# Pair 2's weights and combinations made during the first two pairs of an attention and two-layer kernel, with a rewritten step order and seam

## The chip, the cores and the metric

One core of one Trainium2 chip runs the whole program. The metric is the device time in microseconds (us); lower is better. Engine names are those of the profile: PE (TensorE matmul), PEld (its weight loads), DVE (VectorE), ACT (ScalarE), POOL (GpSimd), SP (SyncE, which issues the DMAs).

## The reference

Rotary attention over 2 batches of 8 heads, 576 positions of 64 values, and then two feed-forward layers over the 1152 tokens (512 values, 2048 hidden). The arithmetic is float32.

```python
attn = softmax(rotate(q) @ rotate(k).T / sqrt(D))     # per head
x = (attn @ v).transpose(0, 2, 1, 3).reshape(1152, 512)
h = x @ w_in                                          # layer 1
x = where(h > 0, h, exp(min(h, 0)) - 1) @ w_out       # elu
h = x @ w2_in                                         # layer 2
out = (h * tanh(softplus(h))) @ w2_out                # mish
```

## The kernel before

Each float32 operand is held as two parts, a rounded high part (a copy by ACT into type fp32r) and a low part (the difference, by DVE or POOL), and each product is three matmuls: high by high, low by high, high by low. XH and XL are the two parts of the layers' input, [128, 4, 1152] (512 values as 4 blocks of 128, then the tokens).

The hidden values of a layer are cut into 16 blocks of 128, taken as 8 pairs. Pairs 0 and 1 of layer 1 are computed plainly, in six units (2 pairs by 3 chunks of 384 tokens): `unit_step(n)` makes `g1_mm` (24 matmuls), `elu` (two ACT passes out of PSUM), `elu_join` (DVE), `elu_hi` (ACT), `elu_lo` (DVE). Units 0 to 2 begin in the end of the attention. After each two units four output tiles wait in `pend`; `g3_mm` makes one (`g2_mm`, 12 matmuls into one of two `ps_h` banks), and `g3_y` copies it into the accumulator Y on ACT.

Pairs 2 to 7 of layer 1 use a scheme of seven products in place of eight. A product `mm(k)`, written P1 to P7 in the step's order, multiplies a combination of weight blocks (a11, a12, s1, a22, s3, s2, s4) with a combination of input blocks (b11, b21, b22 of the input itself, and t1, t2, t3, t4), 12 matmuls of 288 columns. The products accumulate in three PSUM places: "a" and "b" (tag s, two buffers) and "c". The combinations t1 to t4 exist for both batches (u = 0, 1). They are made once, `form1` (three or two elementwise passes of 576 columns out of XH and XL), then `put_hi` (ACT) and `lo1`. t1 is put over a quarter of XH and XL, so it must come after the last unit's matmuls. Pair 2's weight combinations are the object `w2` (class `Pieces`): `load` (an ACT pass out of the raw DMA buffer), `bits` (two or three DVE passes), `sums` (four DVE passes), `round` (high part on ACT, low part on POOL or DVE). `first_pieces(n)` spreads all this over units 2 to 5.

A step of pairs 2 to 7 is the list `STEP`, worked off from left to right by `layer_step`. It is one order for all engines; each engine's queue keeps it, and semaphores join them. P: product; c, d: bank copied out by ACT, or added by DVE, into a temporary (m1, u2, m5, u3, s); e, x, h, l: elu (two ACT passes), join (DVE), high part (ACT), low part; X, K, L: join, high and low part of the previous pair's s; H: one of 12 output tiles of the previous pair (6 matmuls of 384 columns); Y: its sum into Y on DVE; w, p, s, r: load, bits, sums and rounding of the next pair's weights; o, or: bits and rounding of this pair's output weights; a: load of the next output weights. Entries that begin with j have no action. `BY` names the engine of the low parts. In the first step there is no previous pair, and `or0` drains the four output tiles left over in `pend`. A load takes one of three raw buffers, whose next DMA is issued when the last bits pass has read it.

After the sixth step `seam` makes the last pair's 12 output tiles, the high and low parts of the new input (XH, XL from Y), the next weights and combinations; `second` then computes layer 2: three plain chunks (`classic`), then steps of its own order.

Of the kernel before, what the change touches and what calls it, by code (L numbers as in the profile page):

```python
# [14 lines left out]
ALU = mybir.AluOpType  # L15
# [11 lines left out]
def kernel(  # L27
# [196 lines left out]
    def tmp(tag):  # L224
        return late_pool[0].tile([128, 2 * CH], F32, tag=tag, name=tag, bufs=4)

    def tmps():
# [3 lines left out]
        return tmp("ta")  # L231
# [705 lines left out]
    def moe(mp, early):  # L937
# [96 lines left out]
        def g3_y():  # L1034
# [15 lines left out]
        pend, queue1, sums1 = [], [], []  # L1050
# [38 lines left out]
        def unit_step(n):  # L1089
# [35 lines left out]
        def first_pieces(n):  # L1125
            D, G = nc.vector, nc.gpsimd
            if n == 2:
                for u in range(2):
                    for k in range(3):
                        form1(u, "t1", k, G)  # L1130
            elif n == 3:
                for k in range(3):
                    form1(0, "t3", k, G)
                put_hi(0, "t3")
                lo1(0, "t3", G)
                w2.load(0)
                w2.bits(0, 0, 1, 2)
            elif n == 4:
                for k in range(2):
                    form1(0, "t2", k, G)  # L1140
                w2.load(1)
                w2.bits(1, 0, 1, 2)
                put_hi(0, "t2")
                lo1(0, "t2", G)
                for k in range(2):
                    form1(0, "t4", k, D)
                put_hi(0, "t4")
                lo1(0, "t4", D)
                for k in range(3):
                    form1(1, "t3", k, G)  # L1150
                w2.sums(0, 1)
            elif n == 5:
                w2.sums(2, 3)
                w2.round(0)
                w2.round(2)
                put_hi(1, "t3")
                w2.round(3, D)
                w2.round(1, D)
                lo1(1, "t3", D)
                for k in range(2):  # L1160
                    form1(1, "t2", k, D)
                put_hi(1, "t2")
                lo1(1, "t2", G)

# [6 lines left out]
        class Pair:  # L1171
# [28 lines left out]
            def temp(self, nm):  # L1200
                if nm not in self.t:
                    if nm == "s":
                        x = second_pool[0].tile([128, S], F32, tag="sx", name="sx", bufs=1)
# [593 lines left out]
```

## Time and profile before

| | us |
|---|---|
| runs shown, median of 2 (595.70 and 596.48) | 596.09 |
| the profiled execution | 595.98 |
| its span, first to last instruction | 594.2 |
| PE busy in the span | 547.0 |
| DVE busy | 434.5 |
| ACT busy | 341.4 |
| POOL busy | 246.1 |

The profile is of one execution, so a stretch or a wait is read against its span of 594.2 us and its own time of 595.98. Busy time is by engine; the engines run beside each other, so it does not add up to the span. In the trace the attention lies before 158 us, pairs 0 and 1 up to 189.4, the six steps from there to 364.3, the seam up to 391.6 and layer 2 behind it.

### The profile page before, as it was taken

How to read it: one execution, taken by the hardware profiler on the slowest of the kernel's cores; microseconds unless marked ns; L12 is line 12 of the kernel's file. 1: busy time of each engine (PE TensorE's matmuls, PEld its weight loads, DVE VectorE, ACT ScalarE, POOL GpSimd, SP SyncE). 2: the span in 40 equal slices, each digit the busy share in tenths (PEclk: the TensorE clock that was granted, in tenths of full speed). 3: DMA queues.
4: the chain of work that ended last, by engine and by line, in shares of the span. 5: the costliest groups of instructions: out<-in, count | busy, mean ns of one | idle time of the engine just before them, and what ended most of it. 6: DMA issues, size and time to landing. Idle time of an engine off the chain costs nothing.

```text
span 594.2 us, 9329 instructions
## 1 busy us (share of the span) xinstructions
PE 547.0 (92%) x3436; PEld 491.6 (83%) x3436; DVE 434.5 (73%) x736; ACT 341.4 (57%) x640; POOL 246.1 (41%) x196
## 2 busy tenths in 40 slices
PE   9999999999996486999999998596999999999997
PEld 6788888888996386999999997485998988998986
DVE  6677777786635836687887877489688878887764
ACT  4766667787643438476665754355766466455530
POOL 7999989424495304132442323053022132222300
PEclk9999999999999679799999999798999999999999
DMA  6878889644202031314123140210332413213004
GB/s 221 224 179 201 217 217 267 143 138 153 72 0 72 1 107 36 107 35 142 45 98 106 37 142 4 103 36 1 107 107 71 133 48 103 82 61 107 1 1 159
DMA packets 49405, 60.70 MB, mean 102 GB/s; under 512 B 20944, under 2 KB 38736, under 8 KB 48592
## 3 DMA queue, kind: packets, MB, share of 16 engines
q1 hardware_dynamic: 48816, 59.52, 34.3%
q10 hardware_dynamic: 544, 0.59, 0.3%
q8 instruction: 27, 0.44, 0.3%
q14 instruction: 18, 0.15, 0.1%
HBM read 46.92 MB, written 2.36 MB: 83 GB/s over the span
## 4 chain that ended last, share of the span: by engine, by line
PE 77%; DVE 12%; ACT 5%; POOL 3%; issue 2%; DMA 1%; DVEq 0%; ACTq 0%; SPq 0%; POOLq 0%
PE ps_s L1190 23%; PE ps_h L1438 17%; PE ps_h L1028 10%; PE ps_s L478 8%; PE psA L598 7%; PE psT L558 5%; PE ps_h L1011 2%; POOL Y L1083 2%; DVE Y L1042 1%; DVE ta L1239 1%; DVE ta L1083 1%; DVE ws L906 1%; PE ps_s L211 1%; POOL ta L1083 1%; PE psA L667 1%
## 5 line engine op out<-in xcount | busy, mean ns | idle before, releaser
L1210 ACT ACTIVATE ta<-ps_s 128x576 f32<-128x576 f32 x52 | 33.2, 651 | 77.7 <-PE ps_s L1190 77.7
L490 DVE TENSOR_REDUCE mn<-ps_s 128x1 f32<-128x576 f32 x71 | 53.5, 757 | 23.8 <-PE ps_s L478 23.4
L1448 DVE TENSOR_TENSOR Y<-Y,ps_h 128x512 f32<-128x512 f32 (+1 forms) x64 | 43.5, 679 | 26.9 <-PE ps_h L1438 26.6
L512 ACT ACTIVATE P<-ps_s,mn 128x576 f32<-128x576 f32 x71 | 52.4, 739 | 10.7 <-DVE mn L490 9.5
L129 POOL TENSOR_TENSOR wo0bl<-wu,wo0bh 128x512 fp32r<-128x512 f32 x15 | 20.5, 1374 | 89.5 <-ACT wo0bh L128 47.5
L129 POOL TENSOR_TENSOR wo0l<-wu,wo0h 128x512 fp32r<-128x512 f32 x16 | 21.7, 1368 | 78.1 <-ACT wo0h L128 61.4
L1028 PE MATMUL ps_h<-gg,wo0bh 128*128 128x384 f32 x144 | 40.5, 361 | 12.3 <-DVE Y L1042 10.6
L1438 PE MATMUL ps_h<-wo0h,gg 128*128 128x512 f32 x144 | 46.5, 404 | 5.6 <-ACT Y L1446 3.4
L1042 DVE TENSOR_TENSOR Y<-Y,ps_h 128x384 f32<-128x384 f32 x72 | 39.1, 550 | 15.9 <-PE ps_h L1028 15.4
L1438 PE MATMUL ps_h<-wo0bh,gg 128*128 128x512 f32 (+2 forms) x148 | 45.7, 390 | 0.0
L558 PE MATMUL psT<-idn,P 128*128 128x128 f32 x288 | 42.9, 273 | 0.0
L1028 PEld LDWEIGHTS ps_h<-gg,wo0bh 128*128 128x128 f32 x144 | 27.4, 201 | 15.1 <-DVE Y L1042 12.5
L1028 PE MATMUL ps_h<-gg,wo0h 128*128 128x384 f32 x144 | 37.3, 340 | 2.8 <-DVE Y L1042 2.8
L578 ACT ACTIVATE pt<-psT 128x512 f32<-128x512 f32 x40 | 23.8, 594 | 26.0 <-PE psT L558 25.8
L1438 PEld LDWEIGHTS ps_h<-wo0h,gg 128*128 128x128 f32 x144 | 26.6, 192 | 11.5 <-ACT Y L1446 3.9
L598 PE MATMUL psA<-pt,v_t 128*64 128x256 f32 (+1 forms) x240 | 35.9, 401 | 0.0
L558 PEld LDWEIGHTS psT<-idn,P 128*128 128x128 f32 x288 | 34.7, 141 | 1.3 <-DVE mn L490 0.4
L1214 DVE TENSOR_TENSOR ta<-ta,ps_s 128x576 f32<-128x576 f32 x26 | 19.5, 752 | 21.7 <-PE ps_s L1190 21.4
L1438 PEld LDWEIGHTS ps_h<-wo0bh,gg 128*128 128x128 f32 x148 | 26.9, 188 | 5.5 <-DVE Y L1448 0.2
L112 DVE TENSOR_SCALAR wv<-wv 128x512 int32<-128x512 int32 x28 | 14.5, 516 | 22.0 <-ACT wv L96 22.0
L1190 PE MATMUL ps_s<-XH,wi1h 128*128 128x288 f32 x96 | 22.1, 313 | 8.1 <-ACT wi1h L128 8.1
L1438 PE MATMUL ps_h<-wo0l,gg 128*128 128x512 f32 x72 | 29.0, 402 | 0.0
(261 smaller groups left out, 1751.2 us busy)
## 6 DMA issues: line engine op xcount, KB each, us to landing
raw<-in_w_in_dram SPq DMA_DIRECT2D x32, 512.0 KB, 3.7
raw<-in_w_out_dram SPq DMA_DIRECT2D x32, 512.0 KB, 3.7
qk_t<-in_qk_dram SPq DMA_DIRECT2D x6, 1152.0 KB, 5.6
qa<-qh SPq DMA_DIRECT2D x28, 144.0 KB, 3.3
out_dram<-Y SPq DMA_DIRECT2D x8, 256.0 KB, 2.0
ka<-kh SPq DMA_DIRECT2D x14, 144.0 KB, 4.6
ka<-kl SPq DMA_DIRECT2D x14, 144.0 KB, 4.2
qb<-ql SPq DMA_DIRECT2D x14, 144.0 KB, 2.7
```

Of the source, the lines that this page charges most:

```text
L129: (by or nc.gpsimd).tensor_tensor(out=lo, in0=u, in1=plain(hi), op=ALU.subtract)
L478: nc.tensor.matmul(third[j] if us[k] == 2 else psS[us[k]][:, j, :HS], lhsT=l, rhs=r(slice(j * HS, j * HS + HS)), start=(a == 0), stop=(a = ...
L490: nc.vector.tensor_reduce(out=m[:, 0:1], in_=psS[u][:, :, :HS], axis=AX.XY, op=ALU.min)
L512: nc.scalar.activation(out=P.rearrange("p (j n) -> p j n", j=2), in_=s[:, :, :HS], func=AF.Exp, scale=-1.0, bias=m, accum_out=sm_t[p, g][: ...
L558: nc.tensor.transpose(tv[:, c, :], P[:, k:k + 128], idn)
L598: nc.tensor.matmul(o[64 * h:64 * h + 64, cols], lhsT=v, rhs=rhs, start=(c == 0 and first), stop=(c == 4), skip_group_check=True,)
L1028: nc.tensor.matmul(o, lhsT=w[:, e * 128:e * 128 + 128], rhs=x, start=(k == 0), stop=(k == 5))
L1042: nc.vector.tensor_tensor(out=y, in0=y, in1=o, op=ALU.add)
L1190: nc.tensor.matmul(self.o[r][:, u, :H2], lhsT=w[i][:, cc, :], rhs=XO[u][xn][x][:, cc, :], start=(first and n == 0), stop=(last and n == 3 ...
L1210: nc.scalar.activation(out=self.temp(nm), in_=self.bank(r), func=AF.Copy)
L1438: nc.tensor.matmul(o, lhsT=l, rhs=w[:, es], start=(k == 0), stop=(k == 5))
L1448: nc.vector.tensor_tensor(out=y, in0=y, in1=o, op=ALU.add)
```

## The change

The temporaries: tag ta had four buffers of 768 columns, shared by elu, the combinations and the steps, with a buffer of its own for s; now ta has five buffers of 576 and a tag tc one buffer of 768 for elu and the plain chunks of layer 2.

Units: the outputs in `pend` are made one before the join and three before the low part, from unit 2 on. `first_pieces`: t3, t2 and t4 go from POOL to DVE for the most part; w2's load, bits, sums and rounding begin at unit 2; all of t4 is made within unit 5. `STEP` and `BY` are new lists with the same entries; the last step also makes the bits of the next output weights behind their load. `seam`: loads and bits of the weights first, the output weights rounded at once, each g3_y one output behind, the low part of XL one output later than its high part, sums, t3 and t2 inside the loop.

```diff
     def tmp(tag):
-        return late_pool[0].tile([128, 2 * CH], F32, tag=tag, name=tag, bufs=4)
+        n, bufs = (S, 5) if tag == "ta" else (2 * CH, 1)
+        return late_pool[0].tile([128, n], F32, tag=tag, name=tag, bufs=bufs)
...
                 nc.scalar.activation(out=XH[part], in_=Yf[part], func=AF.Copy)
-                (nc.vector if e == 1 or t < 1 else nc.gpsimd).tensor_tensor(
-                    out=XL[part], in0=Yf[part], in1=plain(XH[part]), op=ALU.subtract
-                )
+                late_xl.append((t, e, part))
+            elif late_xl:
+                last_xl()
+
+        def last_xl():
+            t, e, part = late_xl.pop(0)
+            (nc.gpsimd if t and e == 1 else nc.vector).tensor_tensor(
+                out=XL[part], in0=Yf[part], in1=plain(XH[part]), op=ALU.subtract
+            )
...
+                outs(1)
                 o = elu_join(*o)
                 if n == 5:
                     lo1(0, "t1", nc.vector)
                     lo1(1, "t1", nc.vector)
-            if o is not None:
                 o = elu_hi(*o)
-            if n >= 3:
-                outs(4)
-            if o is not None:
+                outs(3)
                 elu_lo(*o)
             first_pieces(n)
...
             if n == 2:
-                for u in range(2):
-                    for k in range(3):
-                        form1(u, "t1", k, G)
+                w2.load(0)
+                w2.load(1)
+                for k in range(3):
+                    form1(0, "t1", k, G)
+                for k in range(3):
+                    form1(0, "t3", k, D)
+                w2.bits(0, 0, 1, 2)
+                w2.bits(1, 0, 1, 2)
+                for k in range(3):
+                    form1(1, "t1", k, G)
+                for k in range(2):
+                    form1(0, "t2", k, D)
             elif n == 3:
-                for k in range(3):
-                    form1(0, "t3", k, G)
+                for k in range(2):
+                    form1(0, "t4", k, D)
+                w2.sums(0, 1, 2, 3)
+                put_hi(0, "t4")
+                lo1(0, "t4", D)
+                w2.round(0)
+                w2.round(1, D)
                 put_hi(0, "t3")
                 lo1(0, "t3", G)
...
                 put_hi(0, "t2")
                 lo1(0, "t2", G)
...
+            elif n == 4:
                 for k in range(3):
-                    form1(1, "t3", k, G)
-                w2.sums(0, 1)
-            elif n == 5:
-                w2.sums(2, 3)
-                w2.round(0)
-                w2.round(2)
-                put_hi(1, "t3")
-                w2.round(3, D)
-                w2.round(1, D)
-                lo1(1, "t3", D)
+                    form1(1, "t3", k, D)
                 for k in range(2):
                     form1(1, "t2", k, D)
+                put_hi(1, "t3")
+                w2.round(2)
+                lo1(1, "t3", D)
+                w2.round(3, D)
                 put_hi(1, "t2")
                 lo1(1, "t2", G)
+            elif n == 5:
+                for k in range(2):
+                    form1(1, "t4", k, D)
+                put_hi(1, "t4")
+                lo1(1, "t4", D)
...
         STEP = (
-            "o00", "P1", "Js", "o10", "Xs", "w0", "cm1", "o01", "p00", "Ks", "P5", "Ls",
-            "p01", "P6", "P2", "cu2", "dm1", "H0", "cm5", "or0", "Y0", "o11", "r0", "H1",
-            "w1", "H2", "em1", "P3", "P7", "cu3", "Y1", "H3", "Y2", "jm1", "p10", "du2",
-            "xm1", "H4", "p11", "d22", "hm1", "P4", "H5", "H6", "s3", "eu2", "Y3", "ju2",
-            "s1", "H7", "xu2", "s2", "eu3", "Y4", "or1", "Y5", "H8", "ju3", "s4", "xu3",
-            "a0", "r1", "Y6", "hu3", "cs", "H9", "Y7", "hu2", "lm1", "H10", "Y8", "Y9",
-            "H11", "Y10", "lu3", "lu2", "Y11", "r3", "r2", "a1", "es",
+            "Js", "P1", "w0", "o00", "cm1", "o01", "P5", "P6", "Xs", "o10", "p00", "Ks",
+            "Ls", "o11", "P2", "or0", "cu2", "H0", "H1", "w1", "p01", "or1", "p10", "dm1",
+            "cm5", "P7", "em1", "jm1", "P3", "Y0", "H2", "p11", "H3", "Y1", "xm1", "s3",
+            "H4", "hm1", "s1", "du2", "Y2", "s2", "H5", "Y3", "cu3", "s4", "H6", "a0",
+            "lm1", "Y4", "H7", "eu2", "Y5", "r1", "P4", "ju2", "xu2", "d22", "r2", "hu2",
+            "eu3", "r0", "H8", "H9", "Y6", "H10", "Y7", "r3", "ju3", "H11", "cs", "xu3",
+            "Y8", "Y9", "lu2", "Y10", "hu3", "Y11", "a1", "es", "lu3",
         )
-        BY = dict(jm1="DVE", js="POOL", ju2="DVE", ju3="POOL", lm1="DVE", ls="DVE", lu2="DVE", lu3="POOL", or0="POOL", or1="POOL", r0="POOL", r1="POOL", r2="DVE", r3="DVE")
+        BY = dict(jm1="POOL", js="DVE", ju2="DVE", ju3="DVE", lm1="POOL", ls="DVE", lu2="DVE", lu3="DVE", or0="DVE", or1="POOL", r0="POOL", r1="POOL", r2="DVE", r3="POOL")
...
                     on[int(r)].load()
+                    if x.q == NF // 2 - 1:
+                        on[int(r)].bits(0, 1, 2)
...
         def seam(x, o):
+            w = ahead_pieces
+            w.load(0)
             x.join("s")
             x.hi("s")
             x.lo("s")
+            w.load(1)
+            w.bits(0, 0, 1, 2)
+            for b in o:
+                b.round()
+            w.bits(1, 0, 1, 2)
             queue1.extend((x, t, e) for t in range(NT // CH) for e in range(NC))
...
+            for i in range(3 * NC):
+                g3_mm()
+                if i:
                     g3_y()
-
-            outs()
-            w.load(0)
-            outs()
-            for b in o:
-                b.bits(0, 1, 2)
-            w.load(1)
...
+                if i == 1:
...
+                    nc.scalar.activation(out=warm, in_=warm, func=AF.Mish)
+                    mish[0] = True
+                if i in (3, 5):
+                    w.sums(*((0, 1) if i == 3 else (2, 3)))
+                if i == 10:
+                    form(0, "t3")
+                    w.round(0)
+                if i == 11:
+                    form(0, "t2")
             g3_y()
-            form(0, "t3")
-            form(0, "t2")
+            last_xl()
             form(0, "t4")
-            w.sums(2, 3)
-            w.round(0)
...
-            for b in o:
-                b.round()
```

## Rows read from the trace of the kernel before

**Rows 1.** The page, parts 1 and 2: busy time by engine; granted clock in 40 slices.

```profile
PE 547.0 (92%) x3436; PEld 491.6 (83%) x3436; DVE 434.5 (73%) x736; ACT 341.4 (57%) x640; POOL 246.1 (41%) x196
...
PEclk9999999999999679799999999798999999999999
```

**Rows 2.** Windows: stretch, its length, busy us (instructions) of each engine, clock, DMA share, GB/s.

```profile
189.40:229.80 40.40, 25.31 (x133) 24.15 (x133) 24.53 (x32) 18.54 (x32) 12.00 (x8) 0.79 0.15 51
229.80:264.30 34.50, 28.48 (x159) 27.34 (x158) 26.32 (x43) 23.95 (x42) 12.63 (x8) 0.85 0.24 76
264.30:289.34 25.04, 23.94 (x157) 23.62 (x156) 20.35 (x37) 15.98 (x28) 8.08 (x5) 1.00 0.27 84
...
364.30:391.60 27.30, 17.19 (x74) 15.05 (x73) 15.79 (x26) 7.50 (x10) 1.85 (x1) 0.81 0.18 60
391.60:415.70 24.10, 18.50 (x93) 16.70 (x92) 23.82 (x26) 14.61 (x24) 11.37 (x7) 0.94 0.06 20
```

**Rows 3.** The chain that ended last: start us, us, engine, tile, line, instructions.

```profile
215.85 8.33 PE ps_h L1011 x48
...
254.07 1.60 PE ps_s L1190 x12
...
302.21 2.08 PE ps_h L1028 x12
```

**Rows 4.** PE's waits, 189 to 416 us: total us, times, longest.

```profile
PE ps_h L1028 <- DVE Y L1042: 13.3, 8, 6.2
PE ps_s L1190 <- ACT wi1h L128: 8.1, 1, 8.1
PE ps_s L1190 <- ACT ta L1210: 7.4, 3, 5.6
PE ps_h L1438 <- ACT Y L1446: 3.4, 1, 3.4
...
PE ps_h L1438 <- DVE gg L1271: 2.2, 1, 2.2
```

**Rows 5.** Timeline of ACT: start us, us, operation, idle before it and releaser.

```profile
191.31 0.68 ACT L997 ACTIVATE xt<-ta 128x576 fp32r<-128x576 f32 x1 [4.42 <-DVE ta L1083]
...
196.81 0.61 ACT L128 ACTIVATE wi1h<-wv 128x512 fp32r<-128x512 f32 x1
...
209.79 0.62 ACT L1210 ACTIVATE ta<-ps_s 128x576 f32<-128x576 f32 x1
```

**Rows 6.** Timelines of DVE and POOL around the first step, columns as in rows 5.

```profile
187.42 1.99 DVE L1083 TENSOR_TENSOR ta<-XH,ta 128x576 f32<-128x576 f32 x1
...
203.93 0.76 DVE L1083 TENSOR_TENSOR ta<-ta,XL 128x576 f32<-128x576 f32 x1
...
159.72 1.42 POOL L1083 TENSOR_TENSOR Y<-XH 128x576 f32<-128x576 f32 x1
...
188.75 1.91 POOL L1083 TENSOR_TENSOR ta<-XH 128x576 f32<-128x576 f32 x1
```

**Rows 7.** Groups of DVE, 289.34 to 314.5: count, busy us, mean ns, idle before.

```profile
L1042 DVE TENSOR_TENSOR Y<-Y,ps_h 128x384 f32<-128x384 f32 x12 | 6.5, 551 | 2.6 <-PE ps_h L1028 2.4
...
L123 DVE SCALAR_TENSOR_TENSOR wu<-raw,wu 128x512 int32<-128x512 int32 x2 | 1.4, 686 | 0.0
...
L906 DVE TENSOR_TENSOR ws<-wv 128x256 f32<-128x256 f32 x2 | 0.8, 418 | 0.0
```

**Rows 8.** Timeline of PE, 282 to 310.

```profile
285.00 0.62 PE L1028 MATMUL ps_h<-gg,wo0bh 128*128 128x384 f32 x2 [1.10 <-DVE Y L1042]
```

**Rows 9.** Timelines of ACT, then of DVE, 364 to 416.

```profile
373.51 0.66 ACT L96 ACTIVATE wv<-raw 128x512 f32<-128x512 f32 x1 [6.42 <-DMA raw<-in_w_in_dram]
...
410.46 1.25 ACT L997 ACTIVATE XH<-gg 128x576 fp32r<-128x576 f32 x2
...
369.02 0.69 DVE L123 SCALAR_TENSOR_TENSOR wu<-raw,wu 128x512 int32<-128x512 int32 x1
...
384.25 0.96 DVE L1046 TENSOR_TENSOR XL<-Y,XH 128x768 fp32r<-128x768 f32 x1 [0.91 <-ACT XH L1045]
```

More of the change, by code (lines that the diff above doesn't have):

```diff
@@ L230, in tmps @@
             return t[:, 0:2 * CH]
-        return tmp("ta")
+        return tmp("tc")
     g_homes = []
@@ L1045, in g3_y @@
                 nc.scalar.activation(out=XH[part], in_=Yf[part], func=AF.Copy)
[L1046 to L1050 removed]
+                late_xl.append((t, e, part))
[6 more added lines that the diff above has]
+            )
+        pend, queue1, sums1, late_xl = [], [], [], []
         late_pool[0] = mp
@@ L1201, in temp @@
                 if nm not in self.t:
-                    if nm == "s":
-                        x = second_pool[0].tile([128, S], F32, tag="sx", name="sx", bufs=1)
-                    else:
-                        x = tmp("ta")[:, 0:S]
-                    self.t[nm] = x.rearrange("p (u n) -> p u n", u=2)
+                    self.t[nm] = tmp("ta").rearrange("p (u n) -> p u n", u=2)
                 return self.t[nm]
@@ L1262, in classic_act @@
             def classic_act(self, t):
-                s = self.t[t] = v2(tmp("ta"))
+                s = self.t[t] = v2(tmp("tc"))
                 nc.scalar.activation(out=s, in_=self.o[t][:, :, :CH], func=AF.Mish)
@@ L1358, in first @@
                 unit_step(n)
-            for k in range(2):
-                form1(1, "t4", k, nc.vector)
-            put_hi(1, "t4")
-            lo1(1, "t4", nc.vector)
             o = [Block(GF + j) for j in range(2)]
@@ L1380, in seam @@
             x.lo("s")
-            queue1.extend((x, t, e) for t in range(NT // CH) for e in range(NC))
-            w = ahead_pieces
-            def outs():
-                if queue1:
-                    g3_mm()
-                if len(sums1) > 1:
-                    g3_y()
-            outs()
-            w.load(0)
-            outs()
-            for b in o:
-                b.bits(0, 1, 2)
-            w.load(1)
-            warm = mp.tile([128, 1], F32, name="warm")
-            nc.gpsimd.memset(warm, 0.0)
-            nc.scalar.activation(out=warm, in_=warm, func=AF.Mish)
-            mish[0] = True
-            outs()
-            w.bits(0, 0, 1, 2)
-            outs()
-            outs()
-            outs()
-            outs()
-            outs()
-            outs()
-            outs()
-            w.bits(1, 0, 1, 2)
-            outs()
-            outs()
-            w.sums(0, 1)
-            outs()
-            outs()
+            w.load(1)
[3 more added lines that the diff above has]
+            w.bits(1, 0, 1, 2)
+            queue1.extend((x, t, e) for t in range(NT // CH) for e in range(NC))
+            for i in range(3 * NC):
+                g3_mm()
+                if i:
+                    g3_y()
+                if i == 1:
+                    warm = mp.tile([128, 1], F32, name="warm")
+                    nc.gpsimd.memset(warm, 0.0)
+                    nc.scalar.activation(out=warm, in_=warm, func=AF.Mish)
[7 more added lines that the diff above has]
+                    form(0, "t2")
             g3_y()
-            form(0, "t3")
-            form(0, "t2")
+            last_xl()
             form(0, "t4")
-            w.sums(2, 3)
-            w.round(0)
             put_hi(0, "t3")
```

11 lines of the change are left out of this document (removed).

## The prediction

> **What bounds the kernel now.** The page gives TensorE (PE) 547 of 594.2 us, 92% of the span; VectorE (DVE) stands at 73% and ScalarE (ACT) at 57%. But the row of granted clock falls below full twice, in slices 12 to 15 and 24 to 26 [rows 1], so PE has two soft places. I read next the stretches, cut where PE changes its work [rows 2]. In a plain step of the first layer, 264.3 to 289.34, PE is busy 23.94 of 25.04 us at clock 1.00: PE bounds it. Four such steps, from the start of that row to the start of the seam's at 364.3, take 100.0 us. The two steps before them take 40.40 and 34.50 us, with PE busy 25.31 and 28.48 and clock 0.79 and 0.85. The seam between the layers, 364.3 to 391.6, has 17.19 busy of 27.30, and the start of the second layer, 391.6 to 415.7, 18.50 of 24.10. The reader sees that the idle time ahead of 416 us that is worth having lies in the two steps, the seam and the start of layer two.
>
> What the work itself needs comes from the chain that ended last [rows 3]: one product of a step (12 matmuls) 1.60 us, two output sums H 2.08 (1.06 each in the plain step), four outputs of the first two pairs 8.33. So the first step (7 products, 4 outputs) needs 11.2 + 8.3 = 19.5 us and the second (7 products, 12 H) 11.2 + 12.7 = 23.9: 43.4 of the 74.9 they take. 31.5 us are lost there.
>
> Who is waited for is in the view of PE's waits [rows 4]: 8.1 us once for the rounded weights of pair 2, 7.4 us in three waits for ACT copies of a bank, 13.3 us in eight for DVE sums into Y (6.2 of it in one, in the seam), and 3.4 and 2.2 us at the start of layer two. ACT's timeline shows why the first comes late [rows 5]: the rounding of pair 2's weights runs at 196.81, behind high parts that wait for combinations on DVE, and the first bank copy of the step, cm1, runs at 209.79. DVE and POOL explain that in turn [rows 6]: a combination of 576 columns takes DVE 0.76 us alone and 1.99 while POOL makes one too.
>
> **Part 1, combinations and weights during the first two pairs (158 to 264.3).** Removed from the way: w2's loads, bits, sums and four roundings now stand at units 2 to 4 instead of 3 to 5, so product P1 finds its weights when unit 5's matmuls end; the 8.1 us wait goes. Its place is taken by what is late next, so I walk the queues, with 0.76 us for a DVE combination alone, 1.9 beside POOL, 0.6 to 0.7 for an ACT pass over 512 or 576 columns [rows 5] and, by width, about 0.85 over 768.
>
> Unit 2: PE comes to it at about 158; the four outputs now stand ahead of unit 3 (158.2 to 166.5, 48 matmuls as in [rows 3]), and two units of 24 matmuls end at 174.8. The total PE work of the units is unchanged. POOL makes the two t1 from 159.7 (six ops, 1.42 alone and 1.91 beside DVE [rows 6]: to about 170) while DVE makes t3 of half 0 at 1.9 each (to about 169), then bits (2.2 us) and t2 (1.5): 173. Unit 3's join is queued behind them on DVE and ends at about 174; its low part at 175.7; t4 177.2; sums 178.9. On ACT the high part of t4, two roundings and two high parts stand ahead of unit 4's elu, whose buffer (tag tc, only one) is no tighter than that: elu runs 180.5 to 182.1, though PE had its bank ready at 174.8. Unit 4's third output needs a PSUM bank that an ACT copy queued behind this elu empties: PE idles 179.1 to 182.6. Unit 5 ends at about 191.7 (its 4.2 us begin at 186.8, with some half clock) instead of 189.4: this stage gets 2.3 us longer.
>
> First step: elu 5 on ACT to 193.4, the join on DVE to 194.3, low parts of both t1 (1.5), low part of unit 5 (1.0), t4 of half 1 (1.5): 198.3; its high part on ACT 199.0; three weight loads queued on ACT behind it (2.0), then cm1: 201.7, against 209.79 + 0.6. P1 and P5 are done by then; P6 and P2 wait for cm1 and, after a gap, run partly at the half clock: 206.5. Now the order drains the four outputs (8.3): 214.8. Behind them on ACT lie the last copy, the rounding, cu2, load, rounding, cm5, em1, hm1, cu3, load, eu2, two roundings, hu2, eu3, two roundings, cs, with one DVE join between: 14.2 us, so the second step's P1 is at 229.0. That is hardly better than 229.8. But in the kernel before the second step then stalled (34.50 us); now its weights are rounded ahead of cs, and cm1 follows cs by five ACT passes (4.1 us), while P1 and P5 run. I give it 26.5: 23.9 + 2.6 of half clock. The third step begins at 255.5 instead of 264.3: -9 us.
>
> Bounds: if DVE is never held up by POOL, unit 4's stall goes and all moves up by some 7 us: -16. If cm1 of the second step stays as late as before and half the stalls return, -3. I take the middle walk, because its ACT sum is made of rows.
>
> The page "SBUF — State Buffer" of the Trainium skill ("SBUF: two separate sides") says that a DVE op with two SBUF inputs and a GpSimd op lock each other out for whole instructions. The 1.99 us row agrees (0.76 plus a wait). If the lock also kept DVE out between POOL's six back-to-back t1 ops, t3 would start at about 168.5 and everything behind it come 1.6 us later; the sum would be 574.6 instead of 573.
>
> **Part 2, the order of the six steps (264.3 to 364.3).** PE's work is the same. Removed: the wait of 1.10 us once a step for a Y sum that is behind a slow join [rows 8]. Per step DVE gains or0's and u3's low parts (0.7 + 0.75) and gives r3's and m1's to POOL (0.4 + 0.75): nothing in sum. New waits to fear: H0 needs u3 and s of the previous pair; lu3 on DVE follows the last H and Y (0.55) and ends 1.3 us into the next step, then two bit ops (1.1), join (0.75), two bit ops (0.85), Ls (0.75): 4.7 us, while H0 is due at 6.4 after four products. Each H needs the Y two before; Y costs 0.55 [rows 7], H 1.06, and small sums stand between them. H4 and H5 have some 0.3 us of room, the rest more. So a step should come to 24.1 to 24.4 instead of 25.0. I take 0.7 per step: -3 us. Bounds: -4 (no wait left) to +4 (1 us lost per step).
>
> **Part 3, the seam (364.3 to 391.6).** In the kernel before an ACT weight load waits 6.42 us for a DMA [rows 9]: SyncE could issue it only when the bits of o, read by DVE at 369.02, freed its raw buffer. XH's high parts stand behind that load on ACT, the low parts and Y sums behind those on DVE, and PE waits 6.2 us. The change takes o's bits into the last step (2.2 us more there, ahead of Y4 and lu3, hidden but for about 1), so the DMA is issued some 15 us earlier. What is then late: low part of s. lu3, bits, join, high, low: about 5 us after the last H. Then weight bits 2.2 us and DVE's own work: 12 Y (6.6), four of six XL at 0.96 (3.8) [rows 9], sums (1.7), t3 and t2 (1.5) = 13.6, about as much as PE's 12.7, so DVE sets the pace. 5 + 2.2 + 13.6 = 20.8, and 21.5 with the roundings that POOL does beside it: -6 us. Bounds -10 (PE's pace) and -2 (XL's on DVE behind their ACT pass make PE wait again).
>
> **Part 4, start of layer two (391.6 to 415.7).** The waits of 2.2 and 3.4 us [rows 4] go back to a DVE queue that is behind: ACT's high parts of t1 stand at 410.46 [rows 9] waiting for it, and Y's copy behind them. In the changed kernel the sums, t3, t2 and two roundings are done inside the loop, so DVE comes out some 4 to 5 us earlier. With the half clock that follows: -5; bounds -7 and 0.
>
> Sum: -9 - 3 - 6 - 5 = -23. Span 594.2 - 23 = 571.2; the profiled execution took 595.98, so 1.8 lie around the span: 573.0. It stands 0.1 under the median of the runs (596.09), which I neglect.
>
> **The rivals.**
> The stall only moves: ACT in the first two steps. For it: after the outputs are drained, 14.2 us of ACT work in one row stand before cs. Against it: each of these passes has a row. Boundary -3, the rest as above: 579.
> The seam is DVE's anyway. For it: 13.6 against 12.7, and 23.82 of 24.10 us busy on DVE after it [rows 2]; against it, 11.5 us of DVE's 27.30 are idle in the seam. -9 - 3 - 2 - 0 = -14: 582.
> Everything fits better (no stall at unit 4, PE's pace in the seam): -16 - 4 - 8 - 7 = -35: 561.
> The other side: the steps. H2 to H7 now run in one row, every H bound to the Y two before, and Y shares DVE with five ops with two SBUF inputs (p11, s3, s1, s2, s4). If each meets one of POOL's now five ops (1.1 to 1.2 us more), a step loses 5.6, four lose 22.4: -20 + 22.4 = +2.4, 598.4. It decides from 5 us a step. Against it: in the plain step the sums and bits on DVE run at an undisturbed 0.42 and 0.69 us [rows 7].
> The change does nothing: that can't be, P1's weights are bound to come sooner; only the gain can be eaten.
>
> **How the numbers follow.** Forecast (its own range 566 to 578) 0.42; the stall only moves 0.18; the seam is DVE's 0.14; better 0.10; the steps lose 0.16. About 2% (11.9 us) is what a measurement of this kernel can tell from no change: 584.2 and 608.0 are the lines. Below the first lie the forecast, the better case, three quarters of the stall case (0.13) and half of the seam case (0.07): 0.72 faster. Above the second lies the steps case only where a step loses 8 us (5.6 + 9.6 / 4): 0.07, with what I have not thought of. Between them 0.21. The range 559 to 590 holds all but the steps case (0.16) and the far end of the better one (0.03).
>
> **What would show it.** Right: no PE wait for wi1h at the start of the first step; cm1 near 202; the third step near 255; steps of 24.1 to 24.4 with no wait for Y; no DMA wait of ACT in the seam, and layer two's first product P1 near 393 instead of 415.7. Wrong: PE waits for Y several times a step; the second step still over 30 us; DVE over 95% busy in the seam with the loop still 27 us.

## The result, and the profile after

| | before | after |
|---|---|---|
| median, us | 596.09 | 574.42 (two runs, 573.49 and 575.36) |
| the profiled execution, and its span | 595.98, 594.2 | 575.36, 573.2 |

The ratio is 0.9637, with an interval of 0.9564 to 0.9709; timed again later over four runs the changed kernel gave 574.51 and 0.9645 (0.9622 to 0.9668). It is 21.7 us faster; 573.0 was forecast. One run of the kernel with unit 4's elu first (1055.73 us) and one of the kernel before beside it (1339.61) are about twice as long as all others and are left out of the ranges and ratios.

The page of the kernel after, parts 1 and 2 (against [rows 1]): the matmuls are the same 3436, PE is busy for 544.3 us of a shorter span, nine operations have gone from POOL to DVE, and the granted clock still has the same two soft places.

```profile
PE 544.3 (95%) x3436; PEld 490.8 (86%) x3436; DVE 436.8 (76%) x745; ACT 342.3 (60%) x640; POOL 221.1 (39%) x187
...
PEclk9999999999999878799999999699999999999999
```

The stretches of the kernel after, cut at the same places as [rows 2] (stretch, its length, busy us and instructions of PE, PEld, DVE, ACT, POOL, granted clock, DMA share, GB/s):

```profile
190.00:228.00 38.00, 29.46 (x156) 27.33 (x154) 19.32 (x28) 19.50 (x34) 6.70 (x5) 0.83 0.18 56
228.00:257.30 29.30, 26.28 (x158) 25.93 (x159) 23.80 (x39) 21.85 (x37) 8.90 (x8) 0.87 0.24 72
257.30:281.00 23.70, 23.70 (x159) 23.70 (x158) 20.04 (x36) 16.21 (x27) 6.03 (x5) 1.00 0.30 90
...
328.50:353.70 25.20, 24.05 (x158) 23.68 (x157) 20.03 (x34) 15.49 (x25) 5.36 (x4) 1.00 0.34 105
353.70:376.30 22.60, 16.05 (x67) 14.46 (x65) 17.21 (x28) 7.25 (x11) 4.85 (x4) 0.77 0.22 70
```

The chain that ended last, of the kernel after (start, us, what): its rows of 48 and 60 matmuls on ps_s are the starts of the steps and of layer two, and 209.15 is the four outputs of the first step ([rows 3]).

```profile
209.15 8.49 PE ps_h L1012 x48
...
257.32 6.34 PE ps_s L1199 x48
...
281.03 6.34 PE ps_s L1199 x48
...
328.46 6.34 PE ps_s L1199 x48
...
395.40 7.93 PE ps_s L1199 x60
```

So the plain step is 281.03 - 257.32 = 23.71 us, and PE is busy in all of it. The gain by stretch:

| stretch | before | after | gain | forecast |
|---|---|---|---|---|
| third step starts at | 264.3 | 257.3 | 7.0 | 9 |
| four steps | 100.0 | 96.2 | 3.8 | 3 |
| seam | 27.3 | 23.9 | 3.4 | 6 |
| start of layer two | 24.1 | 17.9 | 6.2 | 5 |
| rest of layer two | 178.5 | 178.0 | 0.5 | 0 |

The seam is taken from the last output of the last step (353.5) to that of the loop (377.4), the start of layer two from there to the first matmul of P1 in PE's timeline (395.24; 415.66 before). The attention ended some 0.7 us later in this execution (the same row near its end began at 155.62 against 154.90), so the first row is 7.7 net of it.

PE's waits of the kernel after, 150 to 410 us (total, times, longest; against [rows 4]): the 8.1 us for wi1h are gone, Y's 13.3 us in eight waits are 4.1 in three, and all of these lie in the last step and the seam.

```profile
PE ps_s L1199 <- ACT ta L1215: 6.2, 3, 2.7
PE ps_h L1029 <- DVE Y L1043: 4.1, 3, 2.3
PE ps_s L1199 <- ACT wi0h L128: 3.9, 1, 3.9
...
PE ps_h L1012 <- ACT Y L1041: 3.1, 1, 3.1
```

The timeline of ACT of the kernel after (start, us, operation, idle before it and releaser): unit 4's elu, the first bank copy cm1 of the first step ([rows 5] had it at 209.79), and the last 512-column rounding before the second step's first product.

```profile
181.74 0.78 ACT L256 ACTIVATE tc<-ps_s 128x768 f32<-128x768 f32 x1
...
202.79 0.62 ACT L1215 ACTIVATE ta<-ps_s 128x576 f32<-128x576 f32 x1
...
230.28 0.61 ACT L128 ACTIVATE wi0h<-wv 128x512 fp32r<-128x512 f32 x1
```

The seam, where the forecast missed most, is read from three timelines of the kernel after. PE:

```profile
357.39 0.44 PE L1029 MATMUL ps_h<-gg,wo0bh 128*128 128x384 f32 x1 [3.24 <-ACT gg L1249]
...
363.02 1.01 PE L1029 MATMUL ps_h<-gg,wo0bh 128*128 128x384 f32 x2 [2.28 <-DVE Y L1043]
```

DVE, the four passes of weight bits and the sums Y behind them:

```profile
358.05 0.42 DVE L112 TENSOR_SCALAR wv<-wv 128x512 int32<-128x512 int32 x1
358.51 1.82 DVE L123 SCALAR_TENSOR_TENSOR wv<-raw,wv 128x512 int32<-128x512 int32 x1
360.25 1.52 DVE L112 TENSOR_SCALAR wv<-wv 128x512 int32<-128x512 int32 x1
361.81 0.69 DVE L123 SCALAR_TENSOR_TENSOR wv<-raw,wv 128x512 int32<-128x512 int32 x1
362.42 1.01 DVE L1043 TENSOR_TENSOR Y<-Y,ps_h 128x384 f32<-128x384 f32 x2
```

POOL, the low parts of the output weights that the change rounds at once:

```profile
358.50 2.95 POOL L129 TENSOR_TENSOR wo0l<-wu,wo0h 128x512 fp32r<-128x512 f32 x2 [7.90 <-ACT wo0h L128]
```

The two bits passes that ran while POOL ran took 1.82 and 1.52 us, the two outside 0.42 and 0.69. The Y sums wait behind them in DVE's queue, PE waits 2.28 us for Y, and PE's granted clock is at the lower of its two levels (1.2 of 2.4 GHz) until 368.9, as finer stretches of the same kernel show:

```profile
357.40:363.00 5.60, 3.00 (x9) 2.23 (x9) 5.53 (x7) 3.03 (x5) 3.00 (x3) 0.61 0.36 128
363.00:368.90 5.90, 5.88 (x18) 5.88 (x19) 3.08 (x6) 1.68 (x2) 0.00 (x0) 0.50 0.30 91
368.90:377.40 8.50, 7.81 (x44) 7.31 (x44) 6.78 (x13) 2.89 (x5) 1.85 (x1) 1.00 0.01 2
```

The 18 matmuls in 5.9 us are three outputs of 1.97 us each; at full clock two outputs take 2.08 [rows 3].

### The profile page after: what moved, and what is told of

Read it like the earlier page. It is cut to its first block, busy times and chain, and to the rows that moved or that the text cites. A ratio compares the mean times of both kernels' runs of the same rounds, so it can differ in the third digit from the quotient of the medians.

```text
span 573.2 us, 9332 instructions
## 1 busy us (share of the span) xinstructions
PE 544.3 (95%) x3436; PEld 490.8 (86%) x3436; DVE 436.8 (76%) x745; ACT 342.3 (60%) x640; POOL 221.1 (39%) x187
## 4 chain that ended last, share of the span: by engine, by line
PE 78%; DVE 9%; ACT 4%; DMA 3%; issue 3%; SPq 2%; POOL 1%; ACTq 0%; POOLq 0%
PE ps_s L1199 25%; PE ps_h L1426 17%; PE ps_h L1029 12%; PE ps_s L479 6%; PE psA L599 5%; PE psT L559 4%; PE ps_s L211 3%; PE ps_h L1012 3%; DMA raw<-in_w_in_dram 2%; DVE ta L1090 1%; DMA v_t<-in_vp_dram 1%; SPq L380 1%; DVE gg L975 1%; DVE wv L112 1%; PE psA L668 1%
## 5 line engine op out<-in xcount | busy, mean ns | idle before, releaser
L491 DVE TENSOR_REDUCE mn<-ps_s 128x1 f32<-128x576 f32 x71 | 53.5, 757 | 24.1 <-PE ps_s L479 23.9
L1215 ACT ACTIVATE ta<-ps_s 128x576 f32<-128x576 f32 x58 | 37.5, 647 | 53.9 <-PE ps_s L1199 53.9
L1426 PE MATMUL ps_h<-wo0h,gg 128*128 128x512 f32 x144 | 45.3, 396 | 0.9 <-ACT Y L1434 0.9
L129 POOL TENSOR_TENSOR wo0l<-wu,wo0h 128x512 fp32r<-128x512 f32 x13 | 17.6, 1368 | 73.7 <-ACT wo0h L128 55.1
L129 POOL TENSOR_TENSOR wo0bl<-wu,wo0bh 128x512 fp32r<-128x512 f32 x12 | 15.9, 1340 | 64.1 <-ACT wo0bh L128 48.6
L1252 DVE TENSOR_TENSOR gg<-ta,gg 128x576 fp32r<-128x576 f32 x46 | 35.7, 788 | 1.2 <-ACT gg L1249 0.8
L129 POOL TENSOR_TENSOR wi1l<-wv,wi1h 128x512 fp32r<-128x512 f32 x12 | 16.8, 1399 | 43.4 <-ACT wi1h L128 32.9
L1249 ACT ACTIVATE gg<-ta 128x576 fp32r<-128x576 f32 x24 | 16.4, 684 | 24.9 <-DVE ta L1244 24.9
L129 POOL TENSOR_TENSOR wi0l<-wv,wi0h 128x512 fp32r<-128x512 f32 x14 | 19.6, 1400 | 24.8 <-ACT wi0h L128 21.1
```

The source lines that it names most:

```text
L129: (by or nc.gpsimd).tensor_tensor(out=lo, in0=u, in1=plain(hi), op=ALU.subtract)
L491: nc.vector.tensor_reduce(out=m[:, 0:1], in_=psS[u][:, :, :HS], axis=AX.XY, op=ALU.min)
L1215: nc.scalar.activation(out=self.temp(nm), in_=self.bank(r), func=AF.Copy)
L1252: (by or nc.vector).tensor_tensor(out=self.home(nm, 1), in0=self.temp(nm), in1=plain(self.home(nm, 0)), op=ALU.subtract)
L1426: nc.tensor.matmul(o, lhsT=l, rhs=w[:, es], start=(k == 0), stop=(k == 5))
```

## The experiments

**One part undone, or one alone.** The four parts of the sum were tested by putting back one part of the change at a time.

The old order of the steps (STEP and BY of the kernel before, all else as after):

```diff
-            "Js", "P1", "w0", "o00", "cm1", "o01", "P5", "P6", ... "Y11", "a1", "es", "lu3",
+            "o00", "P1", "Js", "o10", "Xs", "w0", "cm1", "o01", ... "r3", "r2", "a1", "es",
-        BY = dict(jm1="POOL", js="DVE", ju3="DVE", lm1="POOL", lu3="DVE", or0="DVE", r3="POOL", ...)
+        BY = dict(jm1="DVE", js="POOL", ju3="POOL", lm1="DVE", lu3="POOL", or0="POOL", r3="DVE", ...)
```

> The changed kernel with the lists STEP and BY of the kernel before; units and seam stay new. Theory (each part pays in its own stretch): the plain steps go back from 23.7 to 24.9 to 25.1 us, three of them +4, and the two first steps lose some 1 to 3 us; 574.4 + 5 to 7 = 579 to 581. Rival (the new order pays mainly in the first two steps, because it drains the four left-over outputs earlier and rounds the next weights ahead of the copy of s): plain steps near 25.0 as well, but the third step begins 8 us or more later, 586 or more. Rival (order is worth nothing): 574 to 576.

579.09 us (578.46 to 581.69), ratio 0.9725: 4.7 us of the gain go. Its plain step takes 25.05 us, and its timeline of PE has the one wait of [rows 8] again in each of them:

```profile
302.53 0.61 PE L1029 MATMUL ps_h<-gg,wo0h 128*128 128x384 f32 x2 [1.10 <-DVE Y L1043]
```

In the changed kernel no wait at all stands between 256 and 328 us. The third step begins at 256.85, 0.5 earlier than after, and that is the attention (the first copy of an elu on ACT behind it began at 158.59, 159.10 after): the new order does nothing for the first two steps, where a loss of 1 to 3 us was expected.

The old seam (its order, its XL behind XH at once, no bits of output weights in the last step):

```diff
-                    if x.q == NF // 2 - 1:
-                        on[int(r)].bits(0, 1, 2)
...
+            queue1.extend((x, t, e) for t in range(NT // CH) for e in range(NC))
+            w = ahead_pieces
+            outs()
+            w.load(0)
+            outs()
+            for b in o:
+                b.bits(0, 1, 2)
```

> The changed kernel with the seam of the kernel before: bits and roundings of the output weights, sums and combinations in their old places, low parts of XL straight behind their high parts, no bits in the last step. Theory (the old seam stalls on the weight load whose DMA waits for those bits): from the last output of the sixth step to the first product of layer two 51 us instead of 41.9, ACT waits 6 us for a DMA, PE 6 us for Y: 574.4 + 9 = 583.5. Rival (with the new step order that DMA is issued early enough anyway): +3 to 5, 577 to 579.

584.37 us (583.73 to 585.48), ratio 0.9808: 9.9 us go, nearly as much as the seam and the start of layer two gain in the table (3.4 + 6.2). The ACT timeline of this kernel has the DMA wait of [rows 9] again, and PE's waits have Y's longest one and those of layer two:

```profile
362.50 0.66 ACT L96 ACTIVATE wv<-raw 128x512 f32<-128x512 f32 x1 [6.87 <-DMA raw<-in_w_in_dram]
```

```profile
PE ps_h L1029 <- DVE Y L1043: 8.2, 4, 5.6
...
PE ps_h L1439 <- ACT Y L1447: 2.3, 1, 2.3
...
PE ps_h L1439 <- DVE gg L1276: 2.1, 1, 2.1
```

The old units (outputs, combinations and w2 of units 2 to 5 as before):

```diff
-                outs(1)
                 o = elu_join(*o)
...
             if n == 2:
+                for u in range(2):
+                    for k in range(3):
+                        form1(u, "t1", k, G)
+            elif n == 3:
+                for k in range(3):
+                    form1(0, "t3", k, G)
+                put_hi(0, "t3")
+                lo1(0, "t3", G)
                 w2.load(0)
```

> The changed kernel with the units and first pieces of the kernel before (combinations mostly on POOL, pair 2's weights rounded after unit 5); order of the steps and seam stay new. Theory (the early weights and combinations are what moves the first two steps): PE waits some 8 us again for the rounded weights of pair 2, and the third step begins 6 to 8 us later: 581 to 583. Rival (the ACT queue of the first step, set by the new order, is the limit either way): +0 to 3, 574 to 577.

581.95 us (580.20 to 582.35), ratio 0.9767: 7.5 us go, the third step begins at 263.94, and the wait of [rows 4] for wi1h is back:

```profile
PE ps_s L1197 <- ACT wi1h L128: 8.1, 1, 8.1
```

The new units and buffers alone, in the kernel before (the edit is shown against that kernel):

```diff
-        return late_pool[0].tile([128, 2 * CH], F32, tag=tag, name=tag, bufs=4)
+        n, bufs = (S, 5) if tag == "ta" else (2 * CH, 1)
+        return late_pool[0].tile([128, n], F32, tag=tag, name=tag, bufs=bufs)
...
+            elif n == 5:
+                for k in range(2):
+                    form1(1, "t4", k, D)
```

> The kernel before with the new units and first pieces alone (and the temporaries' tags); order of the steps and seam stay old. Theory (parts add up): 596.1 - 7 = 589, with P1 of the first step waiting under 2 us. Rival (in the old order the gain is eaten by the second step, whose weights are rounded late): 594 to 596, second step still 33 us or more.

587.93 us (587.25 to 588.11), ratio 0.9863: 7.9 us gained, third step at 255.95, plain steps at 25.06. What goes when a part is undone, 4.7 + 9.9 + 7.5 = 22.1, is the whole of the change's 21.7 within the spread of the runs, and the units are worth the same alone (7.9) as beside the rest (7.5). The parts hardly depend on each other.

**What the half clock costs.** The kernel with the old units runs the changed seam, line for line, but in its execution the clock was back at full at the end of the wait for Y, which was 1.73 us. The same stretches of it as shown above of after (363.00:368.90 of after is 369.8:375.8 here):

```profile
364.30:369.80 5.50, 3.42 (x10) 2.65 (x11) 5.43 (x7) 2.91 (x5) 3.29 (x3) 0.69 0.37 129
369.80:375.80 6.00, 5.31 (x30) 4.93 (x29) 4.58 (x9) 1.69 (x2) 0.00 (x0) 1.00 0.30 87
```

30 matmuls lie here in the time of 18. From the start of the last step to layer two's P1 it takes 64.96 us (335.35 to 400.31), the changed kernel 66.94 (328.46 to 395.40). At the end of the wait the two are only 0.3 us apart (34.24 and 34.56 behind the step's start); the other 1.7 arise behind it, where the clock differs. Two more executions of the same code say how firm that is. The changed kernel in another run has 66.94 again (330.26 to 397.20). The kernel of the next part, which changes nothing from the last step on, waited 2.24 us for Y, as long as the changed kernel, but its clock was back 3.0 us behind the wait, and it takes 65.95 (328.58 to 394.53). First the changed kernel's stretch behind the wait, then that of the other:

```profile
364.80:370.70 5.90, 5.90 (x18) 5.90 (x19) 3.04 (x6) 1.69 (x2) 0.00 (x0) 0.50 0.30 90
```

```profile
362.80:368.70 5.90, 5.56 (x23) 5.24 (x24) 3.54 (x7) 1.68 (x2) 0.00 (x0) 0.75 0.28 89
```

Behind the wait the four take 32.4, 32.4, 31.7 and 30.7 us. So the lower clock there costs up to 1.7 us more in one execution than in another of the same code, and the length of the wait alone does not say how long it stays.

**Can unit 4's stall be had?** The wait of 3.1 us for ACT's copy of Y was forecast as ACT's queue, high parts standing before elu 4. Moved: two roundings and the high parts of t3 and t2, from before elu 4 to behind it.

```diff
+                if n == 4:
+                    outs(1)
+                    w2.round(0)
+                    w2.round(1, nc.vector)
+                    outs(1)
+                    put_hi(0, "t3")
+                    lo1(0, "t3", nc.gpsimd)
...
-                w2.round(0)
-                w2.round(1, D)
-                put_hi(0, "t3")
```

> The changed kernel, but the two roundings and the high and low parts of t3 and t2 that unit 3 queues on ACT stand behind unit 4's elu and between its outputs. Theory (ACT's order alone makes PE wait 3.1 us at unit 4): that wait falls under 1 us, unit 5's matmuls end 2 to 3 us sooner, the first copy of the first step (cm1, 202.8 in the changed kernel) and all behind it move with it: 574.4 - 2.5 = 572. Rival (DVE's combinations pace this stage, so cm1 stays where it is): cm1 within 0.7 us of 202.8, time 574 to 575.

573.79 to 576.51 us over three runs, ratio 0.9632 (0.9595 to 0.9668), as the changed kernel's: no gain. The rows are those of the same kernel in another run.

> Unit 4's elu first, alone, once more for an undisturbed trace. Theory: PE's wait at unit 4 under 1 us, the third step no later than 257. Rival, now the likelier: the wait moves to unit 5 (t1's high part, about 4 us) and cm1 stays at 202 to 203.

574.49 us. PE's timeline of this kernel, and then ACT's:

```profile
181.26 0.62 PE L1012 MATMUL ps_h<-gg,wo0h 128*128 128x384 f32 x2 [0.91 <-ACT Y L1041]
...
195.63 1.18 PE L1203 MATMUL ps_s<-XH,wi1h 128*128 128x288 f32 x2 [4.17 <-ACT XH L998]
```

```profile
191.16 0.68 ACT L998 ACTIVATE xt<-ta 128x576 fp32r<-128x576 f32 x1 [4.36 <-DVE ta L1090]
...
193.34 0.79 ACT L256 ACTIVATE tc<-ps_s 128x768 f32<-128x768 f32 x1
...
202.83 0.64 ACT L1219 ACTIVATE ta<-ps_s 128x576 f32<-128x576 f32 x1
```

The stall's cause was read rightly, 3.1 us became 0.9, but PE then waits 4.2 instead of 1.0 for the high part of t1: ACT sits 4.36 us at a high part that DVE has not fed, and elu 5 and t1 are queued behind it. cm1 comes at 202.83 as before. The stall was not what set cm1. In these rows it is ACT's queue, standing behind a high part that DVE has not fed; whether ACT's order or DVE's row of combinations is to blame they do not show.

**The seam: what sets its first sums.** Low part of s first: the last step's tail makes s's high and low parts directly behind the last outputs.

```diff
+        LAST = STEP[:STEP.index("H11")] + (
+            "H11", "cs", "xu3", "Y8", "es", "Y9", "hu3", "Y10", "xs", "lu3", "hs", "lu2", "Y11", "ls",
+            "a1",
+        )
...
-            x.join("s")
-            x.hi("s")
-            x.lo("s")
```

> The changed kernel; in the sixth step alone the elu of s comes directly behind its copy and its join, high and low part stand ahead of the last Y, and the second output weights' load and bits behind them. Theory (the chain of s on DVE makes PE idle 3.6 us at the seam, and the half clock that follows costs some 4 us more in outputs at 1.9 us each): idle under 1.5 us, the loop runs at full clock for most of its length, 574.4 - 3 to - 7 = 568 to 571. Rival (DVE's work sets the seam's pace, so PE only waits for Y instead): waits for Y grow from 3.0 to 5 us or more and the time stays within 573 to 575.

573.24 us (572.43 to 573.64), ratio 0.9600 (0.9576 to 0.9624): 1.2 less by the median, hardly more than the spread of the runs (the changed kernel's four gave 574.15 to 577.12). The wait for s shrinks (1.53 + 0.28 us instead of 3.24 + 0.35), and the longest one for Y grows to 4.01 us, 5.9 in all. That is what the rival expected (waits for Y of 5 us or more, 573 to 575 us), and not what the theory did. DVE's timeline of this kernel shows the bits beside POOL again, two other passes of them, and Y behind:

```profile
356.49 1.51 DVE L112 TENSOR_SCALAR wv<-wv 128x512 int32<-128x512 int32 x1
358.03 1.63 DVE L123 SCALAR_TENSOR_TENSOR wv<-raw,wv 128x512 int32<-128x512 int32 x1
...
360.64 1.01 DVE L1043 TENSOR_TENSOR Y<-Y,ps_h 128x384 f32<-128x384 f32 x2
```

Then also the bits behind the sums of the second and third output and the roundings, with POOL's part, behind that of the ninth:

```diff
-            w.bits(0, 0, 1, 2)
-            for b in o:
-                b.round()
-            w.bits(1, 0, 1, 2)
...
+                if i in (2, 3):
+                    w.bits(i - 2, 0, 1, 2)
+                if i in (5, 7):
+                    w.sums(*((0, 1) if i == 5 else (2, 3)))
+                if i == 9:
+                    for b in o:
+                        b.round()
```

> As the run before, and besides the bits of the two weights come one by one behind the second and third output of the seam, their sums behind the fifth and seventh, and the rounding of the output weights (POOL) behind the ninth. Theory (bits lengthened by POOL's two low parts, 1.8 and 1.5 us instead of 0.7 and 0.4, hold up the first Y and cost PE 2.3 us): another 1 to 3 us, 566 to 569. Rival (the work only moves behind the loop, where DVE is full already): layer two's first product comes no sooner than in the run before, time within 1 us of it.

571.44 us (571.11 to 571.60), ratio 0.9571 (0.9548 to 0.9594): 3.0 under the changed kernel, 1.8 under the run before. The same passes without POOL beside them, PE's waits, and the last step and seam at full clock:

```profile
358.30 0.42 DVE L112 TENSOR_SCALAR wv<-wv 128x512 int32<-128x512 int32 x1
358.75 0.69 DVE L123 SCALAR_TENSOR_TENSOR wv<-raw,wv 128x512 int32<-128x512 int32 x1
```

```profile
PE ps_h L1029 <- DVE Y L1043: 3.0, 3, 1.2
PE ps_h L1428 <- ACT Y L1436: 2.3, 1, 2.3
```

```profile
353.50:377.00 23.50, 19.86 (x107) 18.21 (x107) 21.10 (x34) 13.27 (x20) 8.95 (x5) 1.00 0.20 68
```

So the bits beside POOL and the lower clock behind PE's waits are what the forecast of the seam lacked; the chain of s it had, at 5 us. This edit takes both away at once, and what each is worth alone it does not show. Part of the gain is lost again: ACT's copy of Y at the start of layer two is now waited for 2.3 us (0.9 after), behind the roundings that were moved there.

**Both together, and further.** Unit 4's reordering and the spread seam in one kernel:

```diff
+                if n == 4:
+                    outs(1)
+                    w2.round(0)
...
+                if i in (2, 3):
+                    w.bits(i - 2, 0, 1, 2)
```

> The three edits of the runs before together. Theory (the stretches are apart, so gains add): 574.4 - 2.5 - 7 = 564 to 568. Rival (one gain is lost to the other or to layer two): 570 or more.

572.15 us (569.03 to 573.12): not under the spread seam alone, so the gains did not add. The wait for t1's high part is there again (4.07 us, at 195.47). Then half 1's high parts of t2 and t3 were moved behind unit 5's as well, with two roundings, and their low parts behind t4:

```diff
+                if n == 5:
+                    put_hi(1, "t2")
+                    put_hi(1, "t3")
...
+                w2.round(2, D)
+                lo1(1, "t2", D)
+                lo1(1, "t3", D)
```

> The three edits together (unit 4's elu first, s early in the sixth step, bits of the seam spread), and besides half 1's high parts of t2 and t3 and two of pair 2's roundings behind unit 5's elu, with their low parts on DVE behind t4. Theory (in the three edits' run the wait at unit 4 only moved to unit 5, 4.1 us for t1's high part, because ACT's elu 5 is queued behind high parts that wait for DVE): that wait falls under 1.5 us, cm1 comes 2 to 3 us sooner than 202.7, 569 to 570. Rival (DVE itself is full from 173 to 203 and paces cm1): cm1 within 0.7 us of 202.7, 571 to 573.

568.95 us (568.24 to 570.33), ratio 0.9545 (0.9526 to 0.9564): 2.5 under the spread seam alone by the medians, but the two intervals overlap. In the trace t1's wait is 0.82, cm1 comes at 200.81 instead of 202.79, and the third step begins at 255.90 (257.15 with the spread seam alone). The edit reorders DVE's row as well as ACT's, so it shows that the order of the two set cm1, not which of them. What the sooner cm1 is worth stays open: in the shortest run of the three edits the third step began as early, at 255.84, with cm1 at 202.68. Last, the first step's copy cs and its rounding stand directly behind P4, and the second step starts with P1, cm1 and then the elu of s:

```diff
+        FIRST = [t for t in STEP if t not in ("cs", "r0", "es")]
+        i = FIRST.index("P4") + 1
+        FIRST[i:i] = ["cs", "r0"]
+        SECOND = ["P1", "cm1", "Es"] + [t for t in STEP if t not in ("P1", "cm1")]
```

> As the run before, and in the first step alone the copy of s and the first rounding directly behind product P4, in the second step the first bank copy cm1 ahead of the elu of s. Theory (the second step's start waits for ACT's queue, 4.5 us for the rounded weights): the wait for wi0h falls under 1.5 us, the second step takes 2 to 3 us less, 566 to 568. Rival (the chain through DVE, add of u3, join, paces the second step; PE then waits for the outputs' operands gg instead): within 1 us of the run before.

567.09 us (566.79 to 569.81), ratio 0.9529 (0.9506 to 0.9552), the shortest of all: 7.3 under the changed kernel. PE's wait for wi0h, 3.9 after, is 1.6 in this kernel, with 1.3 behind it for the low part.

```profile
PE ps_s L1204 <- ACT wi0h L128: 1.6, 1, 1.6
```

The third step begins 5.0 us earlier than without this edit (250.92 against 255.90), but the median gains only 1.9. In the profiled executions the start of layer two's P1 is 3.6 earlier and the span 3.5 shorter; those two were the longest of the one kernel's runs (570.33) and the shortest of the other's (566.79). Of the 5.0, 0.6 is the attention, which ended sooner in this execution (ACT's first elu copy behind it began at 158.49 against 159.14), and part is lost again in the seam, where the granted clock is 0.93 in the mean instead of 1.00 (347.4 to 372.0 here, 352.0 to 376.0 there). The rest is not explained.

The changed kernel itself, timed again beside these two:

> The changed kernel as it is, beside the others on the same chip: 573.5 to 575.5.

574.51 us (574.15 to 577.12), ratio 0.9645 (0.9622 to 0.9668).

## Why the prediction was right, and where it was not

The sum said 573.0 and the runs gave 574.4. It was not as exact as that looks: in the span parts 1 and 3 were too large by 2.0 and 2.6, parts 2 and 4 too small by 0.8 and 1.2, and 0.5 came in the rest of layer two, where nothing was forecast. That they nearly cancelled is luck; that each part moved the way it was forecast to, for the reason given, is not. Two readings of the kernel before were slightly off, and nothing hangs on them. The dips of the clock in [rows 1] are the 14th, 15th and 17th slice (193 to 252 us) and the 26th and 28th (371 to 416). The plain steps took 25.1 to 25.2 us, not 25.0 (they start at 264.37, 289.50, 314.67 and 339.84 in the chain).

**Part 1 (-9 forecast, -7.0, or -7.7 net).** The walk of the queues held in its order and nearly in its times. Unit 4's third output waited as it said, 180.7 to 183.8 (forecast 179.1 to 182.6). Unit 5 ended at 194.1 (191.7), cm1 ran at 202.79 (201.7), the outputs were drained at 217.6 (214.8), P1 of the second step came at 230.94 (229.0), 13.3 us behind them (14.2), and the second step took 26.4 (26.5). P1 of the second step was 1.9 us late: cm1 came 1.1 late, 0.7 of it the attention; 1.7 more arose between cm1 and the drained outputs (209.15 + 8.49 - 202.79 = 14.8 against 13.1), where PE came out of a wait of 2.74 us at the half clock (its 24 matmuls at 203.47 took 5.68 us; 3.18 in a plain step); and ACT's row behind them gave 0.9 back. What was misjudged was the stall at unit 4: it was priced at 2.3 us of the stage, and taking it away by itself gave nothing; cm1 came 2 us sooner only when the next unit's high parts were moved too.

**The lock.** t3 and t1 ran beside each other, DVE and POOL by turns. DVE's rows of the kernel after, and POOL's:

```profile
164.12 1.98 DVE L1090 TENSOR_TENSOR ta<-XH 128x576 f32<-128x576 f32 x1
166.13 3.78 DVE L1090 TENSOR_TENSOR ta<-ta,XL 128x576 f32<-128x576 f32 x2
```

```profile
160.44 1.43 POOL L1090 TENSOR_TENSOR Y<-XH 128x576 f32<-128x576 f32 x1
161.95 3.52 POOL L1090 TENSOR_TENSOR Y<-Y,XL 128x576 f32<-128x576 f32 x2
165.43 1.95 POOL L1090 TENSOR_TENSOR Y<-XH 128x576 f32<-128x576 f32 x1
```

A DVE pass took 1.9 instead of 0.76 and a POOL op 1.95 instead of 1.43: each waits for the other's current op, and neither for the other's row of ops. So DVE did not stay out until POOL's six were done, and the case that would have given 574.6 is not what made 574.4: t3's first pass ran from 164.12 to 166.10, and did not wait for 168.5. The page "SBUF — State Buffer" of the Trainium skill ("SBUF: two separate sides") says that the loser blocks for the whole of the other's instruction; the traces agree, with 1.98 here and 1.82 for the bits in the seam.

**Part 2 (-3 forecast, -3.8; 4.7 when undone).** The step came to 23.71 us, below the 24.1 to 24.4 given: the wait of 1.10 went and nothing took its place. Three plain steps give 1.4 to 1.5 each, of which the wait is 1.10; the last gives 0.5 us back. There the bits put into it ran on DVE at 343.14 for 1.75 us beside POOL's low part (343.05, 1.29 us), and PE waited 1.15 us for Y. The forecast named this, "hidden but for about 1", in its part on the seam, and put it into no sum. The rival in which the steps lose 5.6 each fell: no Y wait was left in a plain step.

**Part 3 (-6 forecast, -3.4).** The DMA wait went as said: no wait of ACT for a DMA is left in the seam (one of 0.7 us stands in the last step, at 334.58), and SP issued the DMA at 344.95, 8.6 us before the seam began. Before, the bits pass that frees its buffer began at 369.02 [rows 9], 4.7 behind the seam's start, so it is some 13 us earlier (forecast 15). What failed is the term of the weight bits. In the sum 5 + 2.2 + 14.3 (DVE's 13.6 and POOL's 0.7), the first measured 4.6 (353.5 to 358.05), the second 4.4 (358.05 to 362.42), the third 15.0 (362.42 to 377.38). So the seam was priced at 21.5 us and took 23.9: the bits were 2.2 longer, the loop 0.7, the chain of s 0.4 shorter. The 2.2 in the sum were their length at DVE's pace alone, while the same change sets POOL's roundings beside them; Part 1 had priced just that meeting. Nor was it priced that PE, having waited 3.24 and 2.28 us, runs at its lower level into the loop; so for 5.9 us it was PE at 1.97 us an output, not DVE, that set the pace. Where the clock came back at once, in the kernel with the old units, the same loop took 13.3 us (369.00 to 382.28) instead of 15.0. The spread seam, with the bits at 0.42 and 0.69 us and the clock at 1.00, is 1.8 us shorter than the run before it, which had both; the rest of the 3.0 came with the earlier s, whose term was not the one that failed.

**Part 4 (-5 forecast, -6.2).** Both waits of [rows 4] at the start of layer two fell, 2.2 to nothing and 3.4 to 0.9, and P1 came at 395.40 (near 393). Its mechanism is tied to the seam: with the old seam both are back at 2.1 and 2.3, and the spread seam, which moves roundings to the loop's end, has ACT's copy waited for 2.3 us again.

Of the rivals, "the seam is DVE's" was half true, for another reason than DVE's own work: its passes beside POOL. "The stall only moves" did not come true in the change, where the third step began 7.0 us sooner; it did, in small, in the run that took the stall at unit 4 away. 574.4 lies in the forecast's own range of 566 to 578.

## What to carry to other kernels

Where an edit puts two streams of elementwise work on DVE and POOL beside each other, price DVE's passes at the length they have next to POOL, also when POOL's side is a rounding that looks free. After each wait of PE that a forecast keeps, price the work behind it at the lower clock too, from a row that shows it. A stall whose cause is read rightly need not be worth its length: ask what sets the next event behind it, since in one order for all engines taking the stall away lets the next wait grow (3.1 to 0.9, 1.0 to 4.2).

## What the runs showed of the hardware that was not expected

A pass with one tensor input was held up beside POOL as well: the 128x512 integer TENSOR_SCALAR took 1.52 us in the seam, 0.42 outside it. Where DVE and POOL each had a row of ops of 576 columns, they went on by turns, at 1.9 us for either's op (0.76 and 1.43 alone), and neither was kept out for longer. After the second wait in the seam PE's granted clock stayed at 0.50 (1.2 GHz) for 5.9 us of work in two executions of the changed kernel. In a third execution of the same code, with a wait as long (2.24 us), it was back at 1.00 after 3.0 us, and in a fourth, with a wait of 1.73, at once. From the last step to layer two's P1 the four took 66.94, 66.94, 65.95 and 64.96 us.
